# Causal attention scores as plain fp32 matmuls on quarters of the array, in tiles of 64 queries of both heads

## Chip, core and metric

The kernel runs on one core of a Trainium2 chip. The time is the device time of one execution in microseconds. The reference's tensors come in and go out in fp32, and the whole program is one launch.

Engine names are those of the profile: PE is the matmul engine (PEld its weight loads), DVE the vector engine, ACT the scalar engine, POOL GpSimd, SP the engine that issues the DMAs.

## The reference

Two attentions over 8 batches, 8 heads, 576 positions and head size 64 are added, and their sum goes into a mixture of four attention experts:

```python
def _attn_ref(q, k, v):                     # [8, 8, 576, 64]
    q_d, k_d, v_d = means of q, k, v over 4 neighbouring positions
    out_d = softmax_attention(q_d, k_d, v_d)              # 144 positions
    out_up = np.repeat(out_d, 4, axis=2)
    mask = np.abs(pos[:, None] - pos[None, :]) < 4         # a band
    out_local = softmax_attention(q, k, v, mask)
    return out_up + out_local

def _moe_ref(x, w_gate, wq, wk, wv, wo):    # x [8, 576, 512]
    logits = x @ w_gate                                    # 4 experts
    w = softmax over the two largest logits of each row
    for e in range(4):
        q, k, v = x @ wq[e], x @ wk[e], x @ wv[e]          # 64 wide
        scores = where(causal, -1e9, q @ k.T / 8)
        a = softmax(scores)
        out += (w of expert e, or 0) * (a @ v @ wo[e])
```

An expert is called a head below; the four make two pairs.

## The kernel before

Everything works on transposed data: channels on the 128 partitions, the 576 positions along the free axis.

**Stage 1** computes the first attention for a batch `b` and a chunk `c` of 128 channels (two of its eight heads). `s1_local` forms the banded scores with plain fp32 matmuls of 64 by 64 on quarters of the array (line 488), `s1_down` those of the averaged positions (546), `s1_out` transposes the softmaxes (587), multiplies with v (602, 616) and writes the sum `x` as a pair `xh`, `xl` whose sum is `x`. Both halves are in the rounded fp32 format fp32r, which the array takes in one pass.

**Stage 2** projects. `project` (645) forms q or k for one pair of heads out of three products (high by high, low by high, high by low) over four chunks, in pieces of 320 and 256 columns, into a large PSUM tile `pj`. `split` then writes q or k as two fp32r halves in SBUF: ACT casts (670), DVE subtracts (671). `s2_v` (704, 713) does v and the gate's logits, `s2_gate` the gate's weights `gw`, and `gt` for the last 64 positions, with one head on the lower and the other on the upper 64 partitions (765).

**Stage 3** is the causal attention. Queries come in tiles of 128, `i` = 0 to 3, and a tail of 64. `s2_scores` gives a tile's two heads one small PSUM tile each: three fp32r matmuls (787) of 64 by 128 for each head, on the two row halves of the array, over the `128 * (i + 1)` keys up to the diagonal block's end. `s2_scores_tail` stacks both heads' 64 queries: `s2_q_tail` (686, 688) copies them into a tile `qz` that is padded with zeros, and six matmuls on the full array (817) follow. For each head, or the tail, DVE scales, masks and takes the maximum (795, 819), ACT exponentiates and sums (793, 824), DVE adds EPS and inverts, GpSimd or DVE multiplies with the inverse and the gate's weight (802, 828). The result is in `pr0` to `pr4`, one buffer each. `s2_trans` transposes 128 by 128 blocks of it on PE (853), 25 for each batch and pair, and ACT or DVE copies them to `pta` (queries 0 to 383) and `ptb` (the others). `s2_av` (899) multiplies with v in plain fp32 on the two column halves; `s2_out` (916), and for the last batch `s2_out_cut` (940), multiply with `wo` and store.

PSUM is in two large tiles (tag `big`: projections, local scores, outputs, the tail's scores) and four small ones (tag `tr`: scores, transposes, v, products with v).

**Order.** The functions above only record operations with their costs and dependencies. `Plan.schedule` (107) simulates the engines and writes one fixed order: each engine takes the operation with the earliest due time whose inputs and buffers are there. Due times follow from the batch and stage (`CYC`, `SHIFT`) and from tables by kind (`LEAD`, `OPL`). On PE it knows four shapes of the array (`MODE`: full, `quarter`, `column`, `row`); it charges `SWC` for a change and keeps to the present shape while such an operation is due within `SWM` us of the earliest (205). Where its model expects the clock to fall, it inserts matmuls on zeros (452).

Of the kernel before, what the change touches and what calls it, by code (L numbers as in the profile page):

```python
# [319 lines left out]
def tile_attn_then_moe(ctx: ExitStack, tc: tile.TileContext, qT, kT, v, wqk, wvg, wo, out):  # L320
# [87 lines left out]
    qz = [cst.tile([128, 2, 128], F32R, name=f"qz{i}") for i in range(NQZ)]  # L408
    for t in qz:
        G.memset(t.bitcast(F32), 0.0)  # L410
    QZ = [Buf(None, None, None, None, None, None) for _ in qz]
# [255 lines left out]
    def split(kind, b, p, w0, x):  # L667
# [2 lines left out]
        op(kind + "_hi", "A", act(576), lambda: A.copy(x()[:, 0, :], ps()[:, H0:H0 + S]), r=[ps], w=[(x, 0)])  # L670
        op(kind + "_lo", "V", dve(576), lambda: V.tensor_tensor(
            x()[:, 1, :], ps()[:, H0:H0 + S], x()[:, 0, :].bitcast(F32), op=OP.subtract),
            r=[ps, (x, 0)], w=[(x, 1)])

    def s2_q(b, p):
        q = QS[b, p] = buf(wk, [128, 2, S], "q", NQ, F32R)
        split("q", b, p, 0, q)

    def s2_q_tail(b, p):

        q, z, Z = QS[b, p], qz[p % NQZ], QZ[p % NQZ]
        for e, r in enumerate(halves):
            def cp(g, e=e, r=r):
                dst, src = z[r, :, 64 * e:64 * e + 64], q()[r, :, 512:S].bitcast(F32)
                if g == "A":
                    A.copy(dst, src)
                else:
                    eng[g].tensor_copy(dst, src)
            op("q_cp", "GAV", (280, 280, 200), cp, r=[q], w=[(Z, e)])

    def s2_k(b, p):
        k = KS[b, p] = buf(wk, [128, 2, S], "k", NK, F32R)
        split("k", b, p, 256, k)
# [39 lines left out]
    def s2_gate(b):  # L733
# [23 lines left out]
        def norm():  # L757
            w, gs, cm = wt(), gst(), cmt()
            V.scalar_tensor_tensor(w, w, 1.5, cm[:, 1, :, 0, :], op0=OP.is_lt, op1=OP.mult)
            V.tensor_reduce(gs[:, 1], w, op=OP.add, axis=AX.X)  # L760
# [2 lines left out]
            V.tensor_tensor(w, w, gs[:, 2, :, None].to_broadcast([128, 5, 4]), op=OP.mult)
            for e, r in enumerate(halves):
                V.tensor_copy(gt()[r], w[hi, 4, :].rearrange("p (a e) -> p e a", e=2)[:, e])
# [2 lines left out]
        op("g_nrm", "V", 1450, norm, r=[cmt], w=[wt, gst, gt])

    PS, PT = {}, {}  # L770

    def s2_scores(b, p, i):
        m = min(128, S - 128 * i)
        n = 128 * i + m
        q, k, gw = QS[b, p], KS[b, p], GW[b]
        if i == order(b)[0]:
            s2_q_tail(b, p)
        if i == 4:
            return s2_scores_tail(b, p)
        pr, (st, ST) = buf(wk, [m, 2, n], f"pr{i}", NPR[i]), rs.next()  # L780
        pss = [small("sq") for _ in range(2)]

        def mm():
            qc = slice(128 * i, 128 * i + m)
            for x, y, one, end in ((0, 0, True, False), (1, 0, False, False), (0, 1, False, True)):
                for e, r in enumerate(halves):
                    T.matmul(pss[e]()[:m, :n], q()[r, x, qc], k()[r, y, :n], start=one, stop=end)  # L787
        op("scores", "T", dense(3, n) + 100, mm, r=[q, k], w=pss, alloc=pss + [pr])
        for e in range(2):
            ps = pss[e]  # L790

            def ex(e=e):
                A.activation(pr()[:, e, :], pr()[:, e, :], AF.Exp, bias=st[:m, e, 4:5], scale=-1.0,  # L793
                             accum_out=st[:m, e, 0:1])
            op("s_max", "V", dve(n) + 4, lambda e=e, ps=ps: V.tensor_tensor_reduce(  # L795
                pr()[:, e, :], ps()[:m, :n], causal[:, 640 - n:640], -0.125, BIG, OP.add, OP.min,
                st[:m, e, 4:5]), r=[ps], w=[(pr, e), (ST, e)])
            op("s_exp", "A", 281 + n / 1.2, ex, w=[(pr, e), (ST, e)])
        op("s_eps", "V", 70, lambda: V.tensor_reduce(st[:, :, 2], st[:, :, 0:2], op=OP.add, axis=AX.X), w=[ST])
        op("s_rec", "V", 83, lambda: V.reciprocal(st[:, :, 3], st[:, :, 2]), w=[ST])  # L800
        for e in range(2):
            op("s_nrm", "GV", (327 + n / 1.2, 189 + n / 1.92), lambda g, e=e: eng[g].tensor_scalar(  # L802
                pr()[:, e, :], pr()[:, e, :], st[:m, e, 3:4],
                gw()[:, i, 2 * p + e:2 * p + e + 1], op0=OP.mult, op1=OP.mult), r=[ST, gw], w=[(pr, e)])
        PS[b, p, i] = pr

    def s2_scores_tail(b, p):

        k, gt = KS[b, p], GT[b]
        pr, (st, ST), ps = buf(wk, [128, S], "pr4", NPR[4]), rs.next(), big("sqt")  # L810
        z = qz[p % NQZ]

        def mm():
            for n0, n1 in ((0, 320), (320, S)):
                dst = ps()[:, H0 + n0:H0 + n1]
                for x, y, one, end in ((0, 0, True, False), (1, 0, False, False), (0, 1, False, True)):
                    T.matmul(dst, z[:, x, :], k()[:, y, n0:n1], start=one, stop=end)
        op("tail", "T", dense(3, 320) + dense(3, 256) + 90, mm, r=[k, QZ[p % NQZ]], w=[ps], alloc=[ps, pr])
        op("s_max", "V", dve(S) + 4, lambda: V.tensor_tensor_reduce(
            pr(), ps()[:, H0:H0 + S], causal_t, -0.125, BIG, OP.add, OP.min, st[:, 0, 4:5]),  # L820
            r=[ps], w=[pr, ST])

        def ex():
            A.activation(pr(), pr(), AF.Exp, bias=st[:, 0, 4:5], scale=-1.0, accum_out=st[:, 0, 0:1])
        op("s_exp", "A", 281 + S / 1.2, ex, w=[pr, ST])
        op("s_eps", "V", 70, lambda: V.tensor_reduce(st[:, 0, 2:3], st[:, 0, 0:2], op=OP.add, axis=AX.X), w=[ST])
        op("s_rec", "V", 81, lambda: V.reciprocal(st[:, 0, 3:4], st[:, 0, 2:3]), w=[ST])
        op("s_nrm", "GV", (327 + S / 1.2, 189 + S / 1.92), lambda g: eng[g].tensor_scalar(
            pr(), pr(), st[:, 0, 3:4], gt()[:, p:p + 1], op0=OP.mult, op1=OP.mult), r=[ST, gt], w=[pr])
        PS[b, p, 4] = pr  # L830

    def s2_trans(b, p, i):
        pr = PS[b, p, i]
        first = []
        if i < 3 and (b, p, 0) not in PT:
            first = [buf(wk, [128, 3, 2, 384], "pta", NPA)]
            PT[b, p, 0] = first[0]
        if i >= 3 and (b, p, 1) not in PT:
            first = [buf(wk, [128, 5, 2, 192], "ptb", NPB)]
# [215 lines left out]
```

## Time and profile before

| | us |
|---|---|
| median of 3 runs | 535.25 (533.56 to 538.29) |
| the profiled execution | 535.31 |
| its span, first to last instruction | 533.4 |
| PE busy | 514.4 (96%) |
| DVE busy | 414.9 (78%) |
| ACT busy | 341.2 (64%) |
| GpSimd busy | 293.7 (55%) |
| mean granted PE clock | 0.990 |

A row of the groups names line, engine, operation, `out<-in` by tiles, shapes and count, then busy us, mean ns of one, the idle time before and who ended it. A row of the timeline or of the chain begins with its start and its length in us and ends with the number of instructions merged in it. A row of the stretches gives the busy time and the instructions of PE, PEld, DVE, ACT and POOL, then the granted PE clock, the DMA share and GB/s.

### The profile page before, as it was taken

The numbers are of one execution on the slowest core, as the hardware profiler recorded it, in microseconds if no ns is written. First come the engines' busy times: TensorE is split into PE (matmuls) and PEld (weight loads), VectorE is DVE, ScalarE is ACT, GpSimd is POOL, SyncE is SP. The second block draws the span as 40 slices with busy tenths as digits, with TensorE's granted clock in tenths as the row PEclk, the third lists the DMA queues.
The fourth block names the chain that finished last, engine by engine and source line by source line (L and its number), as shares of the span: only waits on it lengthen the run. The fifth ranks groups of instructions, "written<-read, shape, count | busy, mean of one in ns | idle before, by whom it ended". The sixth has DMA issues, their size and how long they took to land.

```text
span 533.4 us, 17338 instructions
## 1 busy us (share of the span) xinstructions
PE 514.4 (96%) x6873; PEld 451.5 (85%) x6876; DVE 414.9 (78%) x1248; ACT 341.2 (64%) x1049; POOL 293.7 (55%) x364
## 2 busy tenths in 40 slices
PE   8789989999999999999899999999999999999999
PEld 3568887888899989899798988998898887998886
DVE  6987899978886889968896966988968676537881
ACT  2886566657666656758476656776767475535773
POOL 5499966857755528765344764767474453302220
PEclk9899997999999999999999999999999999999999
DMA  8787744432343117602232323551342010200112
GB/s 208 199 228 191 174 118 116 119 94 55 111 139 93 50 26 216 183 26 68 70 118 81 113 80 106 154 141 50 98 136 70 3 36 1 77 15 12 45 47 89
DMA packets 43584, 52.77 MB, mean 99 GB/s; under 512 B 3312, under 2 KB 26352, under 8 KB 43504
## 3 DMA queue, kind: packets, MB, share of 16 engines
q1 hardware_dynamic: 43504, 51.67, 34.4%
q8 instruction: 54, 0.88, 0.7%
q14 instruction: 26, 0.21, 0.1%
HBM read 41.16 MB, written 9.44 MB: 95 GB/s over the span
## 4 chain that ended last, share of the span: by engine, by line
PE 61%; DVE 23%; POOL 5%; ACT 5%; DMA 2%; issue 2%; POOLq 0%; ACTq 0%; DVEq 0%
PE pj L645 11%; PE po L916 8%; PE o L899 7%; PE pv L704 7%; PE tq L853 6%; PE tp L587 4%; PE sq L787 4%; DVE pr L795 3%; PE o L602 3%; DMA lq<-in_qT_dram 2%; PE sc L488 2%; PE o L616 2%; DVE pr L802 2%; PE scd L546 2%; DVE lp L491 2%
## 5 line engine op out<-in xcount | busy, mean ns | idle before, releaser
L802 POOL TENSOR_SCALAR pr<-pr,pst,gw 128x384 f32<-128x384 f32 (+3 forms) x68 | 48.0, 708 | 72.8 <-DVE pst L800 51.3
L793 ACT ACTIVATE pr<-pr,pst 128x512 f32<-128x512 f32 (+3 forms) x128 | 70.8, 555 | 19.2 <-DVE pst L795 19.1
L645 PE MATMUL pj<-xh,wqk_h 128*128 128x320 f32 (+1 forms) x248 | 77.4, 312 | 0.4 <-DVE lp L491 0.3
L645 PE MATMUL pj<-xl,wqk_h 128*128 128x320 f32 (+1 forms) x248 | 73.2, 295 | 0.0
L645 PE MATMUL pj<-xh,wqk_l 128*128 128x320 f32 (+1 forms) x248 | 73.1, 295 | 0.0
L853 PE MATMUL tq<-ident,pr 128*128 128x128 f32 x400 | 58.6, 276 | 3.9 <-ACT ptb L355 1.5
L795 DVE CUSTOM_DVE_ANT_0 pr<-sq,causal 128x512 f32<-128x512 f32 (+3 forms) x128 | 57.5, 482 | 6.0 <-PE sq L787 4.5
L853 PEld LDWEIGHTS tq<-ident,pr 128*128 128x128 f32 x400 | 45.5, 141 | 8.2 <-ACT ptb L355 2.0
L509 POOL TENSOR_TENSOR lp<-lp,lst 128x640 f32<-128x640 f32 x30 | 38.4, 1283 | 20.6 <-DVE lst L508 10.7
L558 ACT ACTIVATE dp<-scd,dst 128x144 f32<-128x144 f32 x96 | 35.3, 376 | 21.1 <-DVE dst L553 16.9
L645 PEld LDWEIGHTS pj<-xh,wqk_h 128*128 128x128 f32 x248 | 46.7, 188 | 2.2 <-issue 0.6
L645 PEld LDWEIGHTS pj<-xh,wqk_l 128*128 128x128 f32 x248 | 46.8, 189 | 0.0
L645 PEld LDWEIGHTS pj<-xl,wqk_h 128*128 128x128 f32 x248 | 46.6, 188 | 0.0
L787 PE MATMUL sq<-k,q 64*128 64x128 f32 (+3 forms) x384 | 44.3, 345 | 1.2 <-DVE ol L905 0.6
L537 POOL TENSOR_TENSOR lr<-lr 72x512 f32<-72x512 f32 x31 | 40.0, 1292 | 5.0 <-DMA lr<-in_v_dram 4.9
L628 POOL TENSOR_TENSOR xl<-x,xh 128x576 fp32r<-128x576 f32 x29 | 41.4, 1426 | 0.0
L704 PE MATMUL pv<-wvg_h,xh 128*128 128x260 f32 x128 | 38.3, 299 | 1.0 <-DVE pta L357 0.4
L357 DVE COPY pt<-tp 72x384 f32<-72x384 f32 (+2 forms) x63 | 31.4, 518 | 8.6 <-PE tp L587 8.4
L602 PE MATMUL o<-pt,lv 64*64 64x58 f32 (+1 forms) x1280 | 37.0, 230 | 0.4 <-DVE x L623 0.4
L916 PE MATMUL po<-oh,wo_h 128*128 128x320 f32 (+1 forms) x112 | 36.3, 324 | 0.2 <-ACT ot L355 0.2
L704 PE MATMUL pv<-wvg_h,xl 128*128 128x260 f32 x128 | 36.2, 283 | 0.0
L704 PE MATMUL pv<-wvg_l,xh 128*128 128x260 f32 x128 | 36.1, 282 | 0.0
(160 smaller groups left out, 1506.5 us busy)
## 6 DMA issues: line engine op xcount, KB each, us to landing
lv<-in_v_dram SPq DMA_DIRECT2D x64, 160.0 KB
lq<-in_qT_dram SPq DMA_DIRECT2D x32, 292.0 KB
lk<-in_kT_dram SPq DMA_DIRECT2D x32, 292.0 KB
lr<-in_v_dram SPq DMA_DIRECT2D x32, 288.0 KB
out_dram<-ot SPq DMA_DIRECT2D x28, 288.0 KB
wst<-in_wqk_dram SPq DMA_DIRECT2D x1, 1024.0 KB
out_dram<-ot SPq DMA_DIRECT2D x4, 160.0 KB
wst<-in_wvg_dram SPq DMA_DIRECT2D x1, 520.0 KB
```

The source lines that it names most:

```text
L509: op("l_nrm", "GV", (pool_tt(n), dve(n)), lambda e: eng[e].tensor_tensor(p(), p(), st[:, :, 2:3].to_broadcast([128, NT, W]), op=OP.mult), ...
L537: G.tensor_tensor(vr()[:, :, 0:2, :], vr()[:, :, 0:2, :], vr()[:, :, 2:4, :], op=OP.add)
L602: T.matmul(o()[r, 512 * x + z:512 * x + z + n], lv()[kr, t, r], pt()[kr, t - k0, at:at + n], start=True, stop=True)
L628: op("xl", "GV", (1360, dve(576)), lambda e: eng[e].tensor_tensor(xl(), x(), xh()[:, 0:S].bitcast(F32), op=OP.subtract), r=[x, (xh, 0)], w ...
L645: T.matmul(ps()[:, H0 + n0:H0 + n1], ww[:, c, w0 + 128 * p:w0 + 128 * p + 128], xx[b, c]()[:, n0:n1], start=(i == 0), stop=(i == 3 * NP - 1))
L704: T.matmul(ps()[:, :260], xx[b, c]()[:, 128 * t:128 * t + 128], ww[:, c, :], start=(i == 0), stop=(i == 3 * NP - 1))
L787: T.matmul(pss[e]()[:m, :n], q()[r, x, qc], k()[r, y, :n], start=one, stop=end)
L793: A.activation(pr()[:, e, :], pr()[:, e, :], AF.Exp, bias=st[:m, e, 4:5], scale=-1.0, accum_out=st[:m, e, 0:1])
L795: op("s_max", "V", dve(n) + 4, lambda e=e, ps=ps: V.tensor_tensor_reduce(pr()[:, e, :], ps()[:m, :n], causal[:, 640 - n:640], -0.125, BIG, ...
L802: op("s_nrm", "GV", (327 + n / 1.2, 189 + n / 1.92), lambda g, e=e: eng[g].tensor_scalar(pr()[:, e, :], pr()[:, e, :], st[:m, e, 3:4], gw( ...
L853: T.transpose(ps()[:, 128 * x:128 * x + 128], pr()[:, c] if i == 4 else pr()[:, e, c], ident)
L916: T.matmul(ps()[:, H0 + n0:H0 + n1], ww[:, p, 128 * c:128 * c + 128], xx[b, p]()[:, n0:n1], start=(i == 0), stop=(i == 5))
```

## The change

Scores are computed for tiles of 64 queries, `t` = 0 to 8, with both heads stacked on the 128 partitions, and from q and k in plain fp32. A unit `u` = 0 to 4 holds tile 0 alone, or tiles `2u` and `2u - 1`. Each tile takes two matmuls of 64 by 64, one a head; the second tile of a unit puts its heads the other way round, so that a unit's four matmuls lie on the four quarters of the array. Tile 8 lies in a large PSUM tile, the others in small ones.

- q and k are copied from PSUM once (`q_ev`, `k_ev`, on ACT or DVE); `split`, `s2_q_tail` and `qz` go.
- `pr0` to `pr8` are constant tiles of `[128, up to 576]`. Tiles with even `t` have 64 columns more than they fill, which stay zero.
- `gt` now holds the gate's weights for all nine tiles; the normalisation always uses it.
- The transposed tiles split at 320 instead of 384; the product with v treats even and odd tiles apart, as their heads lie in opposite order.
- The output product's two column ranges, 0 to 320 and 320 to 576, wait each for its own columns.
- The planner has `scores` as `quarter`, no special tail, and other due times and parameters.

```diff
-LEAD = {..., "out": 2.1, ...}
+LEAD = {..., "out": 4.2, ...}
-OPL = {... "d_exp": -0.8, "l_rec": 1.4, "l_eps": 2.6, "vd": -4.7, "x": 7.2, "l_exp": 2.0 ...}
+OPL = {... "d_exp": -5.1, "l_rec": 4.4, "l_eps": 6.2, "vd": -2.3, "x": 10.7, "l_exp": -0.5, "k_hi": -1.3, "xt": -2.2 ...}
-WAT, NW0 = (48.0, 24.0, 63.0), 14
-LU, B0 = (1, 2, 3, 8, 10, 12, 15, 16, 24, 26, 28, 30), 2
-ORD, CUT = (2, 3, 4, 1, 0), 256
+WAT, NW0 = (53.0, 30.0, 67.0), 14
+LU, B0 = (1, 3, 8, 10, 12, 13, 16, 22, 24, 28, 29, 30), 2
+ORD, CUT = (3, 4, 2, 1, 0), 320
-LDS, LVL = 5.5, 18.5
+LDS, LVL = 5.9, 17.3
-MODE = {"local": "quarter", "down": "quarter", "o1": "quarter", "o1d": "column", "av": "column", "scores": "row"}
-SWM = {None: 16.3, "quarter": 24.5, "column": 34.1, "row": 13.2}
-SWC, SWB, MARG = 140.0, 0, 36.0
+MODE = {"local": "quarter", "down": "quarter", "o1": "quarter", "o1d": "column", "av": "column", "scores": "quarter"}
+SWM = {None: 17.4, "quarter": 24.5, "column": 34.0, "row": 17.5}
+SWC, SWB, MARG = 140.0, 0, 2.0
...
+    for t in range(NU):
+        pr.append(cst.tile([128, 128 * (t // 2 + 1) if t < NU - 1 else S], F32, name=f"pr{t}"))
...
-    def split(kind, b, p, w0, x):
-        ps = (project_by_pair if (kind, b, p) in PAIRWISE else project)(kind, b, p, w0, [x])
-        op(kind + "_hi", "A", act(576), lambda: A.copy(x()[:, 0, :], ps()[:, H0:H0 + S]), r=[ps], w=[(x, 0)])
-        op(kind + "_lo", "V", dve(576), lambda: V.tensor_tensor(
-            x()[:, 1, :], ps()[:, H0:H0 + S], x()[:, 0, :].bitcast(F32), op=OP.subtract),
...
+    def s2_q(b, p, kind="q", w0=0, to=QS, bufs=NQ):
+        x = to[b, p] = buf(wk, [128, S], kind, bufs)
         ps = (project_by_pair if (kind, b, p) in PAIRWISE else project)(kind, b, p, w0, [x])
+        op(kind + "_ev", "AV", (act(576), dve(576)), lambda e: copy(e, x(), ps()[:, H0:H0 + S]), r=[ps], w=[x])
...
-            V.tensor_tensor(w, w, gs[:, 2, :, None].to_broadcast([128, 5, 4]), op=OP.mult)
+            we = w.rearrange("p t (a e) -> p t e a", e=2)
             for e, r in enumerate(halves):
-                V.tensor_copy(gt()[r], w[hi, 4, :].rearrange("p (a e) -> p e a", e=2)[:, e])
+                for at, src, i0, i1, f in ((0, lo, 0, 4, e), (1, hi, 0, 4, 1 - e), (8, hi, 4, 5, e)):
+                    V.tensor_tensor(gt()[r, at:at + 2 * (i1 - i0) - 1:2, :], we[src, i0:i1, f, :],
+                                    gs[src, 2, i0:i1, None].to_broadcast([64, i1 - i0, 2]), op=OP.mult)
...
+    def s2_scores(b, p, u):
+        q, k, gt = QS[b, p], KS[b, p], GT[b]
+        ts, (st, ST) = unit(u), rs.next()
+        pss = [(big if t == NU - 1 else small)("sq") for t in ts]
+        def part(x, n0, n1):
+            t = ts[x]
+            at = H0 if t == NU - 1 else 0
+            for e, r in enumerate(halves):
+                T.matmul(pss[x]()[halves[e ^ x], at + n0:at + n1], q()[r, 64 * t:64 * t + 64], k()[r, n0:n1],
+                         start=True, stop=True)
+        def mm():
+            part(0, 0, min(320, 64 * ts[0] + 64))
+            if u:
+                part(1, 0, 64 * ts[1] + 64) if u == 4 else None
+                part(0, 320, 64 * ts[0] + 64) if ts[0] > 4 else None
+                part(1, 0, 64 * ts[1] + 64) if u < 4 else None
+        op("scores", "T", 107 * (ts[0] + 1) + 50, mm, r=[q, k], w=pss + [PR[t] for t in ts], alloc=pss)
+        for x, t in enumerate(ts):
...
+            op("s_nrm", "GV", (327 + n / 1.2, 189 + n / 1.92), lambda g, x=x, t=t, n=n: eng[g].tensor_scalar(
+                pr[t][:, 0:n], pr[t][:, 0:n], st[:, x, 3:4], gt()[:, t, p:p + 1], op0=OP.mult, op1=OP.mult),
+                r=[ST, gt], w=[PR[t]])
...
+    def s2_trans(b, p, u):
+        jobs = [(t, j) for t in unit(u) for j in range(t // 2 + 1)]
+        sizes = {0: (1,), 1: (3,), 2: (3, 2), 3: (4, 3), 4: (3, 2, 4)}[u]
+        part = 0 if u < 3 else 1
...
+            out = ob()[:, 0:n].rearrange("p (t q) -> p t q", q=64)
+            for par in range(2):
+                some = [t for t in tiles if t % 2 == par]
+                for j in range(some[-1] // 2 + 1):
+                    ts = [t for t in some if t // 2 >= j]
+                    for e, r in enumerate(halves):
+                        src = pt()[:, j, e ^ par, :].rearrange("p (t q) -> p t q", q=64)
+                        T.matmul(out[r, ts[0] - tiles[0]:ts[-1] - tiles[0] + 1:2, :],
+                                 vg()[:, j, 64 * (2 * p + e):64 * (2 * p + e) + 64],
+                                 src[:, ts[0] - base:ts[-1] - base + 1:2, :], start=j == 0, stop=j == some[-1] // 2)
...
+        for n0, n1 in ((0, CUT), (CUT, S)):
+            op("wo", "T", dense(6, n1 - n0), lambda n0=n0, n1=n1: mm(n0, n1),
+               r=[(x[b, p], n0) for x in (OH, OL) for p in range(2)] + needs(wo_h), w=[ps], alloc=[] if n0 else [ps, ot])
```

More of the change, by code (lines that the diff above doesn't have):

```diff
@@ L376, in tile_attn_then_moe @@
     rd = Ring(NDP, [128, 3, 5], "dst", lambda t: t[:, :, 1:2])
-    causal = cst.tile([128, 640], BF, name="causal")
-    zero = causal[:, 0:512]
+    zero = cst.tile([128, 512], BF, name="zero")
     V.memset(zero, 0.0)
@@ L407, in tile_attn_then_moe @@
     V.memset(lmask[:, NT - 1, S + PADL - SH - 4 * TQ:W], 8 * NEG)
[L408 to L411, printed above, removed]
+    pr, PR = [], []
+    for t in range(NU):
+        pr.append(cst.tile([128, 128 * (t // 2 + 1) if t < NU - 1 else S], F32, name=f"pr{t}"))
+        PR.append(Buf(None, None, None, None, None, None))
+        if t % 2 == 0 and t < NU - 1:
+            G.memset(pr[t][:, 64 * t + 64:], 0.0)
     mlt = cst.tile([128, 4, 4], F32, name="mlt")
@@ L432, in weights @@
             plan.now = at
-            tag, bufs = {id(wqk): ("pta", NPA), id(wvg): ("ptb", NPB), id(wo): ("pr3", NPR[3])}[id(src)]
+            tag, bufs = {id(wqk): ("ptb", NPB), id(wvg): ("pta", NPA), id(wo): ("wos", 1)}[id(src)]
             st = buf(wk, [128, n, m], "wst", bufs, tag=tag)
@@ L665, in project_by_pair @@
         return ps
[L667 removed]
+    def s2_q(b, p, kind="q", w0=0, to=QS, bufs=NQ):
+        x = to[b, p] = buf(wk, [128, S], kind, bufs)
         ps = (project_by_pair if (kind, b, p) in PAIRWISE else project)(kind, b, p, w0, [x])
[L670 to L689 removed]
+        op(kind + "_ev", "AV", (act(576), dve(576)), lambda e: copy(e, x(), ps()[:, H0:H0 + S]), r=[ps], w=[x])
     def s2_k(b, p):
[L692 to L693 removed]
+        s2_q(b, p, "k", 256, KS, NK)
     def s2_v(b, t):
@@ L766, in s2_gate @@
         op("g_rank", "V", 1230, rank, r=[vg], w=[wt, gst, cmt], alloc=[wt, gst, cmt, gt])
         op("g_exp", "A", 230, ex, w=[cmt])
[L768 to L781, printed above, removed]
-        def mm():
[L784 to L830, printed above, removed]
@@ L832, in s2_trans @@
-    def s2_trans(b, p, i):
-        pr = PS[b, p, i]
-        first = []
[L835 to L839, printed above, removed]
-            PT[b, p, 1] = first[0]
-        part, q0 = (0, 128 * i) if i < 3 else (1, 128 * i - 384)
-        pt = PT[b, p, part]
-        m = min(128, S - 128 * i)
-        jobs = [(j, e) for e in range(2) for j in range(i + 1)] if i < 4 else [(j, 0) for j in range(5)]
-        per = {0: 2, 1: 4, 2: 3, 3: 4, 4: 4}[i]
-        for g in range(0, len(jobs), per):
-            js = jobs[g:g + per]
+        op("g_nrm", "V", 1650, norm, r=[cmt], w=[wt, gst, gt])
@@ new lines, in s2_trans @@
+    def s2_trans(b, p, u):
+        jobs = [(t, j) for t in unit(u) for j in range(t // 2 + 1)]
+        sizes = {0: (1,), 1: (3,), 2: (3, 2), 3: (4, 3), 4: (3, 2, 4)}[u]
+        part = 0 if u < 3 else 1
+        first = []
+        if (b, p, part) not in PT:
+            first = [buf(wk, [128, 3, 2, CUT], "pta", NPA) if part == 0 else buf(wk, [128, 5, 2, S - CUT], "ptb", NPB)]
+            PT[b, p, part] = first[0]
+        pt = PT[b, p, part]
+        for size in sizes:
+            js, jobs = jobs[:size], jobs[size:]
@@ L848, in s2_trans @@
             ps = small("tq")
+            ts = sorted(set(t for t, _ in js), reverse=True)
             def tr(js=js, ps=ps):
-                for x, (j, e) in enumerate(js):
-                    c = slice(min(128 * j, S - 128), min(128 * j, S - 128) + 128)
-                    T.transpose(ps()[:, 128 * x:128 * x + 128], pr()[:, c] if i == 4 else pr()[:, e, c], ident)
-            es = sorted(set(e for _, e in js))
-            o = op("trans", "T", 109 * len(js) + 5, tr, r=[pr] if i == 4 else [(pr, e) for e in es], w=[ps],
-                   alloc=[ps] + first)
+                for x, (t, j) in enumerate(js):
+                    c = min(128 * j, pr[t].shape[1] - 128)
+                    T.transpose(ps()[:, 128 * x:128 * x + 128], pr[t][:, c:c + 128], ident)
@@ L857, in s2_trans @@
+            o = op("trans", "T", 109 * size + 5, tr, r=[PR[t] for t in ts], w=[ps], alloc=[ps] + first)
             if not first:
@@ L887, in s2_av @@
         oh, ol = OH[b, p], OL[b, p]
-        jobs, rd = [], [vg]
-        for part, (a, z) in enumerate(((0, 384), (384, S))):
-            a0, z0 = max(a, qlo), min(z, qhi)
-            if a0 < z0:
-                rd += [(PT[b, p, part], (i, g)) for i in range(5) if a0 <= 128 * i < z0 for g in range(10)]
-                js = [j for j in range(5) if 128 * j < z0]
-                jobs += [(PT[b, p, part], a, j, max(a0, 128 * j), z0, j == 0, j == js[-1]) for j in js]
-        def mm():
-            for pt, a, j, q0, q1, one, end in jobs:
-                for e in range(2):
-                    T.matmul(ob()[64 * e:64 * e + 64, q0 - qlo:q1 - qlo],
-                             vg()[:, j, 64 * (2 * p + e):64 * (2 * p + e) + 64],
-                             pt()[:, j, e, q0 - a:q1 - a], start=one, stop=end)
-        n = qhi - qlo
-        op("av", "T", cost, mm, r=rd, w=[ob], alloc=al)
+        part = int(qlo >= CUT)
+        pt, base, n = PT[b, p, part], part * CUT // 64, qhi - qlo
+        tiles = range(qlo // 64, qhi // 64)
+        cost = 30 + 110 * sum(t // 2 + 1 for t in tiles)
+        def mm():
+            out = ob()[:, 0:n].rearrange("p (t q) -> p t q", q=64)
[8 more added lines that the diff above has]
+                                 src[:, ts[0] - base:ts[-1] - base + 1:2, :], start=j == 0, stop=j == some[-1] // 2)
+        rd = [(pt, (t, j)) for t in tiles for j in range(5)]
+        op("av", "T", cost, mm, r=[vg] + rd, w=[ob], alloc=al)
         op("o_hi", "A", act(n), lambda: A.copy(oh()[:, qlo:qhi], ob()[:, :n]), r=[ob], w=[(oh, qlo)])
@@ L972, in stage3 @@
                 p, i = sched[x]
-                yield "scores", (0.35, 0.5, 0.65, 0.85, 0.8)[i], s2_scores, (b, p, i)
+                yield "scores", (0.17, 0.35, 0.55, 0.8, 1.0)[i], s2_scores, (b, p, i)
             if x > 0:
                 p, i = sched[x - 1]
-                yield "trans", (0.22, 0.44, 0.65, 0.87, 0.55)[i], s2_trans, (b, p, i)
+                yield "trans", (0.11, 0.33, 0.55, 0.76, 0.98)[i], s2_trans, (b, p, i)
                 if i in cuts:
-                    yield "av", cuts[i][2] / 1e3, s2_av, (b, p) + cuts[i]
+                    yield "av", 1.0 if cuts[i][0] == 0 else 1.8, s2_av, (b, p) + cuts[i]
         if last:
-            for n0, n1, cost in ((CUT, S, 816), (0, CUT, 653)):
+            for n0, n1, cost in ((CUT, S, 653), (0, CUT, 816)):
                 for c in range(NP):
```

71 lines of the change are left out of this document (39 added, 32 removed).

## Prediction

> **What bounds the kernel now.** I read first the engine shares and the granted clock on the page, then the busy time by stretch.
>
> ```profile
> PE 514.4 (96%) x6873; PEld 451.5 (85%) x6876; DVE 414.9 (78%) x1248; ACT 341.2 (64%) x1049; POOL 293.7 (55%) x364
> ...
> PEclk9899997999999999999999999999999999999999
> ...
> 0.00:80.00 80.00, 69.84 (x1148) 54.89 (x1151) 65.57 (x169) 51.58 (x175) 58.81 (x76) 0.97 0.75 186
> 80.00:520.00 440.00, 432.24 (x5644) 387.26 (x5644) 347.79 (x1074) 285.22 (x864) 234.41 (x287) 0.99 0.28 83
> 520.00:533.40 13.40, 12.29 (x88) 9.32 (x84) 1.59 (x5) 4.45 (x12) 0.51 (x1) 1.00 0.25 88
> ```
>
> The columns after the stretch are PE, PEld, DVE, ACT and POOL. From 80 to 520 us PE is idle for 7.76 of 440 us while DVE has 79% and ACT 65%: there the time is what PE has to do. In the first 80 us PE is idle for 10.2 us, with DVE at 82% and the DMA engines at 75%.
>
> A busy PE is not one that streams all the time, so next I read its timeline, in start times:
>
> ```profile
> 267.17 0.28 PE L916 MATMUL po<-oh,wo_l 128*128 128x256 f32 x1
> 267.28 0.28 PE L916 MATMUL po<-ol,wo_h 128*128 128x256 f32 x1
> 267.49 1.15 PE L787 MATMUL sq<-k,q 64*128 64x256 f32 x12
> 268.57 0.42 PE L645 MATMUL pj<-xh,wqk_h 128*128 128x320 f32 x1
> 268.82 0.31 PE L645 MATMUL pj<-xh,wqk_l 128*128 128x320 f32 x1
> 268.97 0.31 PE L645 MATMUL pj<-xl,wqk_h 128*128 128x320 f32 x1
> ...
> 7.26 0.34 PE L488 MATMUL sc<-lk,lq 64*64 64x64 f32 x8
> ...
> 525.92 0.39 PE L940 MATMUL po<-oh,wo_h 128*128 128x256 f32 x1
> ```
>
> L916 comes every 0.11 us, but 0.21 passes from its last to the first score matmul: 0.10 to leave a shape of the array. L645 comes every 0.15, but its second is 0.25 behind its first: 0.10 to enter one. I went through all start times and counted where the shape changes (full array, rows halved, columns halved, quarters): 232 changes, from the one at 7.26 to the one at 525.92. The runs between them are 76 full, 56 quarter, 52 column and 49 row runs. The excess over an operation's usual interval, on both sides of each change, without single excesses over 0.25 us (those are waits), sums to 37.6 us: **0.16 us a change**.
>
> **The score matmuls: 0.** From the chain of work, which shows how far each group moves PE on:
>
> ```profile
> 258.33 2.86 PE o L899 x32
> ...
> 261.70 0.59 PE sc L488 x40
> ...
> 262.51 0.50 PE scd L546 x12
> ...
> 263.71 0.48 PE sq L787 x6
> ...
> 267.56 1.08 PE sq L787 x10
> ...
> 273.12 1.17 PE sq L787 x12
> ...
> 505.58 0.80 PE sqt L817 x6
> ```
>
> Before, for a batch and pair: tile 0 is 0.48, tiles 1 and 2 are 1.08, tile 3 with another tile 0 is 1.17, the tail 0.80. Taking 0.16 for a change off the first two, the set is 0.32 + 0.92 + (1.17 - 0.48) + 0.80 = 2.73 us. After, a plain fp32 matmul has two records (L488 issues 20 matmuls and shows 40), so two passes. A unit holds two tiles on the four quarters; its time is that of the longer: 64, 192, 320, 448 and 576 columns, 1600 in all, 3200 with both passes. L488 runs four at a time: 10 rounds of 64 columns in 0.59, 0.92 ns a column. L546 has 144 columns and 4 rounds in 0.50: 0.87. L899, also plain fp32, takes 2.86 for 3200 column-passes in pieces of 64 to 384; less one change, 0.84. The new streams are of that length, so I take 0.84: 2.70 us. Over 16 sets this saves 0.5 us, which I count as 0; at L488's price it would be 2.94 and add 3.4 us in all.
>
> This rests on four matmuls side by side. L546 decides that: one matmul after another, each second pass beginning with the next one's first, would make 7 steps of 0.125, 0.87 us; the row has 0.50, four steps. [...]
>
> **Changes of shape: -5.1 us.** With quarter scores the row shape goes. Keeping the order and only renaming the 64 score operations of L787 from rows to quarters leaves 206 changes; renaming the tail too, 220 (a full-array operation among full ones becomes an island). Leaving all scores out, 168: the floor, if each found a quarter run that is there anyway. The planner holds a quarter run while its next operation is due within 24.5 us, and now has 80 more operations for such runs, so I take 200: 32 x 0.16 = 5.1 us. Ends: 220 (1.9) and 168 (10.2).
>
> **q and k not split, softmax on fewer columns: -2.0 us.** Rows of the groups:
>
> ```profile
> L671 DVE TENSOR_TENSOR q<-pj,q 128x576 fp32r<-128x576 f32 x16 | 12.0, 749 | 6.5 <-ACT q L670 6.4
> L671 DVE TENSOR_TENSOR k<-pj,k 128x576 fp32r<-128x576 f32 x16 | 12.0, 748 | 2.3 <-ACT k L670 2.2
> L670 ACT CAST q<-pj 128x576 fp32r<-128x576 f32 x16 | 10.2, 639 | 5.7 <-PE pj L645 5.6
> L355 ACT COPY ot<-po 128x576 f32<-128x576 f32 x18 | 11.5, 636 | 6.5 <-PE po L916 4.8 <-issue 1.3 <-ACT pr L793 0.2
> L795 DVE CUSTOM_DVE_ANT_0 pr<-sq,causal 128x512 f32<-128x512 f32 x32 | 21.1, 681 | 0.5 <-PE sq L787 0.3
> L795 DVE CUSTOM_DVE_ANT_0 pr<-sq,causal 128x128 f32<-128x128 f32 x32 | 8.1, 282 | 3.6 <-PE sq L787 2.2 <-POOL lp L509 1.4
> L793 ACT ACTIVATE pr<-pr,pst 128x512 f32<-128x512 f32 x32 | 22.8, 715 | 3.6 <-DVE pst L795 3.5
> L793 ACT ACTIVATE pr<-pr,pst 128x128 f32<-128x128 f32 x32 | 12.7, 397 | 6.2 <-DVE pst L795 6.2
> ```
>
> Each of 32 projections loses a cast (0.64) and a subtraction (0.75) and gains one copy (0.64): 24 us less on DVE and ACT together, and the projection's PSUM tile, one of two large ones, is free 0.75 earlier. Nine maxima, exponentials and normalisations stay for each pair, over 2880 columns instead of 3136: at (681-282)/384 = 1.04 ns that is 4.3 us of DVE, at 0.83 ns 3.4 us of ACT. All of it lies beside PE and costs or saves nothing by itself; what it can reach are PE's 7.76 us of idle time after 80 us. These rows show who ends PE's waits:
>
> ```profile
> PE tp L587 <- POOL lp L509: 3.4, 4, 1.3
> ...
> PE tq L853 <- ACT ptb L355: 1.5, 1, 1.5
> ```
>
> No single engine ends most of it, and POOL's local softmax is not touched, so I take a quarter: 2.0, between 0 and 5.
>
> **The passage at 73 to 86 us: -1.7 us.** After 21 us the clock fell once:
>
> ```profile
> 73.00:80.00 7.00, 5.50 (x97) 4.77 (x95) 6.82 (x22) 3.88 (x15) 3.87 (x5) 0.92 0.19 54
> 80.00:83.50 3.50, 3.08 (x59) 2.10 (x61) 3.37 (x11) 1.14 (x4) 1.48 (x3) 0.50 0.01 2
> 83.50:87.00 3.50, 3.50 (x58) 3.20 (x52) 2.99 (x10) 2.28 (x8) 1.37 (x2) 0.69 0.26 70
> ...
> 73.73 0.66 DVE q L671
> 74.49 0.97 DVE qz L688
> ...
> 78.03 0.74 DVE gw L759
> ```
>
> The third column from the end is the granted clock: 0.92 of 7 us, 0.50 and 0.69 of 3.5 us each, together 3.4 us of PE's time lost. Before it DVE is the chain, with q's subtraction and a copy into the padded tail tile: 1.63 us that go. Whether PE's load then stays high enough to hold the clock the trace can't say: half of 3.4. Ends: all of it, or a second such fall, +3.4.
>
> **The rest on PE: +0.5 us.** Transposes stay 25 a pair. The product with v has 28 matmuls instead of 16, the same 1600 columns; 24 more passes at a few ns (0.92 against 0.84 ns on 64 columns is 5 ns a pass) are 0.1 us a pair, partly hidden: 0.5 to 2. The copies of transposed tiles go from 8 to 10 a pair on ACT or DVE, hidden by their slack; uncovered, 32 x 0.3. Memsets, constants and the new due times cost nothing: they lie in the first 60 us, behind the loads. The output product now waits for its own columns of both pairs alone, which can only start it earlier.
>
> **Gates: 0, but see the rivals.** The normalisation of the gates loses a product and two copies and gains six products on 64 partitions:
>
> ```profile
> L763 DVE TENSOR_TENSOR gw<-gw,gs 128x20 f32<-128x20 f32 x8 | 2.3, 293 | 0.3
> L765 DVE COPY gt<-gw 64x2 f32<-64x2 f32 x16 | 3.8, 240 | 0.4
> ```
>
> Six at 0.24 to 0.29 less 0.77 make 0.7 to 1.0 us a batch on DVE.
>
> **Sum.** The profiled execution took 535.31 us (span 533.4), the median is 535.25: the same. 535.3 - 5.1 - 2.0 - 1.7 + 0.5 = **527.0 us**, 1.5% less.
>
> **Rivals.**
> - *Reshaping doesn't fall.* Score units are released by the four small PSUM tiles, not by what the array is doing; 49 row runs for 64 operations speak for that. Then 220 changes remain, the idle time moves elsewhere, and with the copies uncovered nothing is left: 531 to 537.
> - *All of it comes.* 168 to 180 changes, the clock holds, 4 us of idle time close: 535.3 - 9.5 - 4 - 3.4 = 518.
> - *The gates take over, slower.* Until now only the tail needed the rearranged gates; now all nine tiles do, so the first normalisation comes 6 x 0.27 - 0.29 = 1.3 us later wherever it waits for the gates. DVE works through the products in order, with the maxima queued behind them; ACT, the transposes and PE wait in turn. The chain at 73 to 79 us runs through the gates already. If all eight batches wait: +10.6, less 1.9 for the least reshaping: 544. It decides as soon as a unit's sums are ready before the last gate product; against it speaks that PE's waits name the gates only once, for 0.6 us:
>
> ```profile
> PE sq L787 <- DVE gs L760: 0.6, 1, 0.6
> ```
>
> [...]
>
> **Numbers.** Less than 1%, 5.4 us, is about what a measurement tells from no change here. Forecast, 523 to 529.9: 0.38. All of it, below 523: 0.20. No fall, 530 to 540.6: 0.23. Gates: 0.16. Order: 0.03. So faster 0.58, same 0.23, slower 0.19. The range goes from 516, the gain with the floor of 168 changes and the idle time nearly closed, to 544, the gates' price.
>
> **What would show it.** Right: no 64-row by 128-column matmul is left; about 200 changes of shape; a pair's score units move PE by about 2.7 us beside the changes; the clock stays at 1.0 from 20 us on; DVE and ACT are together 20 to 30 us less busy. Wrong: score rows that take over 3.2 us a pair; PE idle over 8 us between 80 and 520; waits of transposes on the gates or on the normalisation; a second dip of the clock.

## Result and the profile after

The changed kernel takes 521.1 us (median), against 534.7 for the kernel before in four runs: 0.9725 of the time before by the means (95% interval 0.9663 to 0.9787). One of its own four runs took 795.9 us; that slow run is left out of the ratio. Forecast were 527.0 us and a range of 516 to 544. The profiled execution has a span of 519.5 us, 13.9 less than before.

The engine shares and the granted clock on its page:

```profile
PE 503.0 (97%) x7468; PEld 447.8 (86%) x7468; DVE 392.0 (75%) x1256; ACT 331.2 (64%) x1049; POOL 276.4 (53%) x346
...
PEclk9899998999999999999999999999999999999999
```

The busy time by stretch (PE, PEld, DVE, ACT, POOL, then clock, DMA share, GB/s):

```profile
0.00:80.00 80.00, 72.44 (x1273) 57.11 (x1273) 67.03 (x183) 49.62 (x167) 63.10 (x84) 0.98 0.78 194
80.00:508.00 428.00, 420.01 (x6120) 382.78 (x6121) 324.49 (x1073) 277.99 (x873) 213.33 (x263) 1.00 0.29 84
508.00:519.50 11.50, 10.58 (x78) 7.93 (x76) 0.49 (x1) 3.62 (x9) 0.00 (x0) 1.00 0.30 104
```

PE is busy 11.4 us less, DVE 22.9, ACT 10.0 and POOL 17.3 less. PE's idle time in the middle stretch has not fallen: 8.0 of 428 us, against 7.8 of 440.

Counted from PE's start times as in the prediction, the changes of shape fell from 232 to 176 (66 full, 63 quarter and 48 column runs), their excess from 37.9 to 27.7 us; excesses over 0.25 us, the waits, from 22.7 to 19.5. (The first figure was 37.6 in the prediction, without three single operations between two changes.) The numbers of changes are firm; the sizes depend on what is taken as an operation's usual interval. With the median of each group's intervals the excess falls by 7 us instead of 10. From one start to the next, all score matmuls move PE by 50.1 us in all, before by 42.0 for the tiles and 14.2 for the tails.

The second fall of the clock is still there, half as long:

```profile
78.00:82.00 4.00, 2.50 (x53) 1.79 (x49) 3.91 (x18) 3.07 (x13) 3.34 (x4) 0.93 0.76 218
82.00:86.00 4.00, 3.91 (x77) 2.33 (x73) 3.17 (x11) 2.69 (x8) 3.37 (x6) 0.65 0.69 168
```

7% and 35% of 4 us are 1.7 us lost, against 3.4 before.

This accounting puts half to three quarters of the gain (7 to 10 of 13.6 us) on the changes of shape. But the chain of work says something else beside it. Its shares by engine, first of the kernel before, then of the changed one:

```profile
PE 61%; DVE 23%; POOL 5%; ACT 5%; DMA 2%; issue 2%; POOLq 0%; ACTq 0%; DVEq 0%
```

```profile
PE 74%; DVE 20%; ACT 3%; issue 2%; POOL 1%; ACTq 0%; DVEq 0%; POOLq 0%
```

DVE has a fifth to a quarter of the chain, though PE is 96% busy. So there are three candidates for the cause that the experiments can separate: fewer changes of shape, less work on DVE, and the new tables of the planner.

### The profile page after: what moved, and what is told of

It is laid out like the page before. It is cut to its first block, busy times and chain, and to the rows that moved or that the text cites. A ratio compares the mean times of both kernels' runs of the same rounds, so it can differ in the third digit from the quotient of the medians.

```text
span 519.5 us, 18547 instructions
## 1 busy us (share of the span) xinstructions
PE 503.0 (97%) x7468; PEld 447.8 (86%) x7468; DVE 392.0 (75%) x1256; ACT 331.2 (64%) x1049; POOL 276.4 (53%) x346
## 4 chain that ended last, share of the span: by engine, by line
PE 74%; DVE 20%; ACT 3%; issue 2%; POOL 1%; ACTq 0%; DVEq 0%; POOLq 0%
PE pj L647 15%; PE pv L687 8%; PE o L854 8%; PE tq L815 8%; PE po L871 7%; PE sq L770 6%; PE tp L589 5%; PE o L604 3%; DVE pr L783 3%; PE o L618 2%; PE sc L490 2%; PE scd L548 2%; DVE lp L493 2%; DVE pr L794 2%; PE pv L696 2%
## 5 line engine op out<-in xcount | busy, mean ns | idle before, releaser
L794 POOL TENSOR_SCALAR pr<-pr,pst,gt 128x64 f32<-128x64 f32 (+8 forms) x86 | 59.6, 699 | 105.2 <-DVE pst L791 40.5
L786 ACT ACTIVATE pr<-pr,pst 128x384 f32<-128x384 f32 (+7 forms) x144 | 80.0, 556 | 33.0 <-DVE pst L783 32.4
L647 PE MATMUL pj<-xh,wqk_h 128*128 128x320 f32 (+1 forms) x248 | 76.6, 309 | 1.4 <-DVE lp L493 0.6
L783 DVE CUSTOM_DVE_ANT_0 pr<-sq,causal_t 128x384 f32<-128x384 f32 (+7 forms) x144 | 66.3, 481 | 12.4 <-PE sq L770 12.0
L647 PE MATMUL pj<-xl,wqk_h 128*128 128x320 f32 (+1 forms) x248 | 73.2, 295 | 0.0
L647 PE MATMUL pj<-xh,wqk_l 128*128 128x320 f32 (+1 forms) x248 | 73.1, 295 | 0.0
L770 PE MATMUL sq<-k,q 64*64 64x320 f32 (+5 forms) x704 | 56.7, 397 | 0.1
L647 PEld LDWEIGHTS pj<-xh,wqk_h 128*128 128x128 f32 x248 | 46.6, 188 | 4.3 <-DVE x L625 1.3
L647 PEld LDWEIGHTS pj<-xh,wqk_l 128*128 128x128 f32 x248 | 46.7, 188 | 0.0
L647 PEld LDWEIGHTS pj<-xl,wqk_h 128*128 128x128 f32 x248 | 46.6, 188 | 0.0
L511 POOL TENSOR_TENSOR lp<-lp,lst 128x640 f32<-128x640 f32 x29 | 37.0, 1278 | 16.5 <-DVE lst L510 14.0
L860 DVE TENSOR_TENSOR ol<-o,oh 128x320 fp32r<-128x320 f32 (+1 forms) x32 | 14.6, 456 | 34.7 <-ACT oh L859 34.4
L770 PEld LDWEIGHTS sq<-k,q 64*64 64x64 f32 x704 | 29.0, 134 | 11.2 <-DVE pst L783 1.0
L604 PEld LDWEIGHTS o<-pt,lv 64*64 64x64 f32 x1280 | 30.9, 135 | 7.1 <-issue 3.1
L630 POOL TENSOR_TENSOR xl<-x,xh 128x576 fp32r<-128x576 f32 x26 | 36.9, 1421 | 0.0
L359 DVE COPY pt<-tp 72x384 f32<-72x384 f32 (+2 forms) x57 | 28.5, 515 | 11.2 <-PE tp L589 11.0
```

The lines of the kernel that those rows point to most:

```text
L511: op("l_nrm", "GV", (pool_tt(n), dve(n)), lambda e: eng[e].tensor_tensor(p(), p(), st[:, :, 2:3].to_broadcast([128, NT, W]), op=OP.mult), ...
L604: T.matmul(o()[r, 512 * x + z:512 * x + z + n], lv()[kr, t, r], pt()[kr, t - k0, at:at + n], start=True, stop=True)
L630: op("xl", "GV", (1360, dve(576)), lambda e: eng[e].tensor_tensor(xl(), x(), xh()[:, 0:S].bitcast(F32), op=OP.subtract), r=[x, (xh, 0)], w ...
L647: T.matmul(ps()[:, H0 + n0:H0 + n1], ww[:, c, w0 + 128 * p:w0 + 128 * p + 128], xx[b, c]()[:, n0:n1], start=(i == 0), stop=(i == 3 * NP - 1))
L770: T.matmul(pss[x]()[halves[e ^ x], at + n0:at + n1], q()[r, 64 * t:64 * t + 64], k()[r, n0:n1], start=True, stop=True)
L783: op("s_max", "V", dve(n) + 4, lambda x=x, t=t, n=n, src=src: V.tensor_tensor_reduce(pr[t][:, 0:n], src(), causal_t[:, S - n:S], -0.125, B ...
```

## Experiments

Times are medians of several runs; a ratio is to the kernel before, on the same chip. Each chip's kernel before had a median of 533.0 to 534.7 us. Changes, excess and waits (both in us) are from start times, as above, in the one profiled execution of each kernel.

| kernel | us | ratio (95%) | changes | excess | waits |
|---|---|---|---|---|---|
| before | 534.7 | 1 | 232 | 37.9 | 22.7 |
| changed | 521.1 | 0.973 (0.966-0.979) | 176 | 27.7 | 19.5 |
| e1 quarter | 526.3 | 0.983 (0.977-0.990) | 176 | 27.3 | 25.0 |
| e2 full | 532.6 | 0.997 (0.995-0.999) | 306 | 49.7 | 13.8 |
| e3 second copies | 527.8 | 0.987 (0.983-0.991) | 176 | 27.0 | 25.9 |
| e4 old tables | 533.1 | 0.998 (0.996-1.000) | 194 | 29.2 | 28.8 |
| e5 before, new tables | 540.9 | 1.012 (1.007-1.017) | 246 | 39.6 | 26.3 |
| e6 before, moved | 543.6 | 1.017 (1.011-1.024) | 243 | 39.6 | 28.8 |
| e7 changed, moved | 539.7 | 1.010 (1.007-1.013) | 192 | 29.0 | 33.5 |
| e8 gates | 527.9 | 0.987 (0.982-0.992) | 176 | 27.9 | 24.4 |
| e9 before, moved again | 545.4 | 1.022 (1.017-1.027) | 242 | 38.2 | 29.6 |
| e10 changed, moved again | 528.2 | 0.990 (0.985-0.995) | 182 | 28.6 | 28.0 |
| e11 light | 514.7 | 0.966 (0.961-0.971) | 176 | 27.2 | 17.8 |
| e12 refit | 520.5 | 0.976 (0.971-0.981) | 176 | 27.4 | 20.2 |

### What a change of shape costs: e1 and e2

e1, ahead of a score unit's matmuls:

```diff
+            T.matmul(pss[0]()[lo, H0:H0 + 64] if ts[0] == NU - 1 else pss[0]()[lo, 0:64], zero[lo, 0:64], zero[lo, 0:64], start=True, stop=True)
             part(0, 0, min(320, 64 * ts[0] + 64))
```

> The changed kernel with one bf16 matmul of zeros on one quarter (64 by 64, 64 columns) ahead of each of the 80 score units; it writes columns that the unit then overwrites, and the order is the same. Control for the next run. All theories: 80 x 0.03 to 0.06 us, so 521 to 526.

e2, the same on the full array:

```diff
+            T.matmul(pss[0]()[:, H0:H0 + 64] if ts[0] == NU - 1 else pss[0]()[:, 0:64], zero[:, 0:128], zero[:, 0:64], start=True, stop=True)
             part(0, 0, min(320, 64 * ts[0] + 64))
```

> The same with the matmul of zeros on the full array, so that a quarter run is broken ahead of the unit: in the written order 61 units follow a quarter operation (two changes of shape more), 8 a column operation (one more), 11 a full one (none): 130 more. Theory 'changes of shape are the gain', 0.16 us each: 21 us above the control, 543 to 547. Rival 'the gain is relief of DVE and ACT, PE would only have waited': less than 8 us above the control.

The control lost 5 us, but in the profiled execution not by its matmuls: the first projection of batch 0 (L662) began 4 us later, long before the first matmul of zeros at 66.7 us. Its rows in the view of that line, of the changed kernel, e1 and e2; the second time is the first start:

```profile
L662 PE MATMUL pj<-xh,wqk_h x8: 279/294/413, 40.6 to 46.0; 128*128 128x320 f32 x4, 128*128 128x256 f32 x4
```

```profile
L662 PE MATMUL pj<-xh,wqk_h x8: 279/292/416, 44.6 to 49.9; 128*128 128x320 f32 x4, 128*128 128x256 f32 x4
```

```profile
L662 PE MATMUL pj<-xh,wqk_h x8: 279/292/421, 41.0 to 46.5; 128*128 128x320 f32 x4, 128*128 128x256 f32 x4
```

From there to the end of the span it is 478.9 us in the changed kernel, 524.0 - 44.6 = 479.4 in e1 and 530.7 - 41.0 = 489.7 in e2. So the matmuls themselves cost 0.5 us, 0.006 each against the 0.03 to 0.06 of the expectation, which was an estimate, and 130 changes cost **10.3 us, 0.08 each**, in which lies also what a full matmul takes more than a quarter one. This rests on one execution each; the fastest runs of e1 and e2, 520.6 and 531.3, are 10.7 apart. By the medians, the measure set beforehand, the difference is 6.3, with late starts of the control in it: that is under the rival's 8. By either measure the theory's 21 us are out, by half or more.

The excess did rise, by 22 us in the table's count and by 19 with the groups' medians: 0.15 to 0.17 a change. The rest was made up elsewhere. The table's count finds it in waits, which fell by 11; with the medians it lies in intervals too short to count as waits. That PE came later to work that then was ready fits both, but is not shown by itself.

```profile
PE 83%; DVE 13%; ACT 2%; issue 1%; POOL 0%; DVEq 0%; ACTq 0%; POOLq 0%
```

In e2's chain DVE's share is down to 13%, from 20% in the changed kernel: where PE is slower, DVE gives less of the length.

### What DVE's work costs: e3 and e11

e3 gives DVE a second copy behind each copy of q or k:

```diff
+        def ev(e):
+            copy(e, x(), ps()[:, H0:H0 + S])
+            V.tensor_copy(x(), ps()[:, H0:H0 + S])
-        op(kind + "_ev", "AV", (act(576), dve(576)), lambda e: copy(e, x(), ps()[:, H0:H0 + S]), r=[ps], w=[x])
+        op(kind + "_ev", "AV", (act(576), dve(576)), ev, r=[ps], w=[x])
```

> The changed kernel with a second copy of q and k on DVE behind the first, for each of 32 projections: 24 us of DVE and 0.8 us more from a projection to its scores, as the split had; order and changes of shape as in the changed kernel. Theory 'changes of shape': 521 to 526, DVE work lies beside PE. Rival 'relief of DVE and ACT': most of the gain goes, 529 to 535.

527.8, 6.6 above the changed kernel, between the two. The rows of the second copies:

```profile
L675 DVE COPY k<-pj 128x576 f32<-128x576 f32 x16 | 12.1, 756 | 8.4 <-ACT k L357 8.1
L675 DVE COPY q<-pj 128x576 f32<-128x576 f32 x16 | 12.1, 755 | 12.2 <-ACT q L357 11.8
```

As the copies came late in a fixed order, this alone could be the order's disturbance. e11 goes the other way, with the order as it is; it leaves out half of each sum and maximum, so it does not compute the result:

```diff
-... V.tensor_reduce(st[:, :, 0], p(), op=OP.add, axis=AX.X)
+... V.tensor_reduce(st[:, :, 0], p()[:, :, 0:W:2], op=OP.add, axis=AX.X)
-... scs[x]()[:, 0:n * SD].rearrange("p (t w) -> p t w", w=SD),
+... scs[x]()[:, 0:n * SD].rearrange("p (t w) -> p t w", w=SD)[:, :, 0:SD:2],
```

> The changed kernel with less work on DVE and the order as it is: the sum of the banded softmax and the maximum of the averaged one are taken over every second column only (the other half is left out), 64 and 32 instructions of half the length: about 20 us less of DVE, as q and k not being split took off. Theory 'relief of DVE is worth little, its work lies beside PE; the second copies cost because they came late in a fixed order': 518 to 521. Rival 'DVE's work sets the time': 513 to 516.

514.7: 6.4 less, the rival's number. The groups and the chain of e11, with the two groups of the changed kernel first:

```profile
L508 DVE TENSOR_REDUCE lst<-lp 128x10 f32<-128x640 f32 x32 | 25.8, 808 | 2.9 <-ACT lp L507 2.4 <-ACT lp L501 0.5
...
L552 DVE TENSOR_REDUCE scd<-scd 128x2 f32<-128x288 f32 x64 | 24.1, 381 | 3.4 <-PE scd L548 3.1
```

```profile
L552 DVE TENSOR_REDUCE scd<-scd 128x2 f32<-128x144 f32 x64 | 17.1, 269 | 4.7 <-PE scd L548 4.1
L508 DVE TENSOR_REDUCE lst<-lp 128x10 f32<-128x320 f32 x32 | 15.2, 475 | 3.2 <-ACT lp L507 2.7 <-ACT lp L501 0.4
```

```profile
PE 76%; DVE 15%; ACT 4%; issue 2%; DMA 1%; POOL 1%; SPq 0%; ACTq 0%; DVEq 0%; POOLq 0%
```

17.6 us less on these two groups gave 6.4 us; 24 us more (32 x 0.75) cost 6.6: **about 0.3 us for 1 us of DVE, in both directions**, at the same 176 changes. The price is rough. e11 ran where the kernel before took 533.0 instead of 534.7 us; set against the kernel before on the same chip, e11 gains 4.7 and e3 loses 7.1 us, 0.27 and 0.30 for 1 us. And DVE's busy time as a whole moved less than the groups, by 14.6 and 19.0 us; by it the prices are 0.32 to 0.44. The intervals of e11 and the changed kernel touch. But both signs hold, and my theory falls here: DVE's work doesn't lie beside PE. The chain had said as much. 20% of 519.5 us are 104 of DVE's 392 busy us, 0.27 of each.

### The planner's tables: e4, e5, e6, e7, e9, e10

e4 is the changed kernel with `LEAD`, `OPL`, `WAT`, `LU`, `SHIFT`, `LDS`, `LVL`, `SWM` and `MARG` of before; e5 is the kernel before with the new ones.

> The changed kernel with the due times and planner constants of before (all tables but the order of the last batch and its cut). The written order has 193 changes of shape instead of 175. Theory 'changes of shape': 18 x 0.17 = 3 us more, 523 to 526. Rival 'the new tables are the gain, not the quarters': 531 to 536.

> The kernel before with the due times and planner constants of the changed one (all tables but the order of the last batch and its cut); 245 changes of shape in the written order instead of 231. Theory 'tables fit one code only; the quarters give what is left at equal fit': worse than before, 537 to 545. Rival 'the new tables are better for any code and are the gain': 520 to 528.

e4 lost 12 of the 13.6 us; the rival's number. Yet e5 is 1.2% slower than before, so the new tables aren't better in themselves. e6 and e9 (before) and e7 and e10 (changed) move each entry of `OPL` by a random amount of at most 0.3 us, which is enough for another order; in e7:

```diff
-OPL = {"s_nrm": 3.2, "l_nrm": 4.2, "t_ev": 1.0, "tp_ev": 6.1, ...}
+OPL = {"s_nrm": 3.042, "l_nrm": 3.962, "t_ev": 0.938, "tp_ev": 5.893, ...}
```

> The kernel before with each entry of OPL moved by a random amount of at most 0.3 us: the fit of its tables is spoiled, nothing else (242 changes of shape instead of 231). Theory 'tables fit one code only': 538 to 545, and about 10 above the changed kernel with spoiled or old tables (533). Rival 'the tables of before are no special fit': 533 to 537, and the changed kernel with old tables at 533 says that the quarters give nothing.

> The changed kernel with each entry of OPL moved by a random amount of at most 0.3 us (191 changes of shape instead of 175). Theory 'tables fit one code only': 527 to 534, like the run with the old tables. Rival 'the new tables are good in a wide surrounding': 520 to 524.

> The kernel before with another random movement of OPL by at most 0.3 us (241 changes of shape). So far spoiled tables gave 540.9 and 543.6 for the kernel before, 533.1 and 539.7 for the changed one: 5.9 apart in the means, 13 with fitted tables. Theory 'at equal fit the quarters give about 8, the rest of the 13 is the fit': 539 to 545. Rival 'the fit is all': the same as the next run within 2 us.

> The changed kernel with another random movement of OPL by at most 0.3 us (181 changes of shape). Theory 'at equal fit the quarters give about 8': 530 to 537, with the excess at changes of shape near 28 us and the rest of the loss in PE's waits. Rival 'the fit is all': the same as the run before within 2 us.

e7 was slower than expected, e10 faster, e9 just above its bound. With tables not made for the code the kernel before takes 540.9, 543.6 and 545.4, the changed one 533.1, 539.7 and 528.2: means of 543.3 and 533.7, **9.6 apart** (standard error 3.6 from three and three). With their own tables they are 13.6 apart. All three of the changed kernel lie below all three of the kernel before. So the change probably holds without the fit; from three and three, a 95% interval would still reach 0. The fit is worth about as much as the change: 9 us on the kernel before, 13 on the changed one. It can be seen where: among the kernels before the excess at changes is 38 to 40 us, among the changed ones 27 to 29, fitted or not; what the fit takes away are waits, 23 and 19 us instead of 26 to 34.

### Gates: e8

```diff
-            for e, r in enumerate(halves):
+            for e, r in [x for x in enumerate(halves) for _ in range(2)]:
```

> The changed kernel with the six gate products done twice on DVE, so that every normalisation of a batch may start 1.4 us later; same order. Rival of the prediction 'the gates' chain sets the time': 8 x 1.4 = 11 us more, 530 to 533. Theory 'it lies beside PE': 521 to 524.

527.9, 6.8 more, for 6.4 us of DVE:

```profile
L749 DVE TENSOR_TENSOR gt<-gw,gs 64x8 f32<-64x8 f32 (+1 forms) x96 | 12.8, 160 | 1.7
```

One product takes 0.16 us, so the delay was 1.0 a batch, not 1.4. The loss is as long as the work, but in the profiled execution it came almost whole through the clock, which fell twice more, each time to 0.66 over 5 us, 1.7 us lost, and longer after 82 us:

```profile
82.00:90.00 8.00, 7.06 (x106) 4.92 (x107) 7.18 (x28) 5.52 (x16) 6.70 (x10) 0.57 0.53 139
143.00:148.00 5.00, 4.43 (x22) 4.01 (x23) 4.23 (x12) 3.41 (x14) 4.19 (x6) 0.66 0.46 138
198.00:203.00 5.00, 5.00 (x114) 4.37 (x114) 3.76 (x10) 2.68 (x13) 2.66 (x3) 0.66 0.60 172
```

43% of 8 us are 3.4 us lost in the first of these rows, against 1.7 in the changed kernel: together 5.1 us more. From the first projection, at 42.0 us, to the end e8 takes 484.4 us, 5.5 more than the changed kernel. That leaves 0.4 us beside the clock. The mean granted clock is 0.984 to 0.990 in all four runs of e8 and 0.993 to 0.997 in three of the changed kernel, so the falls belong to e8 and not to one execution. The gates hold up POOL's normalisation in four places in both kernels (9.6 us in all, 13.3 in e8), not in every batch, and no wait of PE is put down to them.

### Another fit: e12

e12 has other values in `OPL`, `LEAD`, `SHIFT`, `SWM` and `LU`.

> The changed kernel with other due times, planner constants and choice of local softmaxes, found by a random search for the earliest end in the planner's own model (2.2 us earlier than for the changed kernel; 175 changes of shape). Theory 'the fit to the planner's model is worth what it says': 518 to 521. Rival 'a gain of 2 us in the model is drowned by what it leaves out': 521 to 530.

520.5, within the first theory's bounds; its interval of 0.971 to 0.981 can't be told from that of the changed kernel. No version here that computes the whole result is clearly faster.

## Why the prediction was right, and where it was off

**Direction and range** held: faster, 521.1 within 516 to 544, by 2.5% (medians) to 2.75% (means) instead of 1.5%. But 521.1 lies below the band of 523 to 529.9 that had the greatest chance; the rival "All of it comes", with a chance of 0.20, had the nearest number, 518. Of its conditions the 176 changes came, while the clock fell again and PE's idle time didn't close. The sum fell 5.3 us short of the gain, nearly all of it in the term for DVE.

**Score matmuls, 0.** Right as far as it can be told: 50.1 us instead of 56.2, both with the changes among them; no run has the streams alone. The quarters work side by side, and more freely than assumed. Two cuts of the changed kernel's PE groups by shape, at the start of a unit that is issued as 320, 128, then 384 columns:

```profile
L770 PE MATMUL sq<-k,q 64*64 64x384 f32 x2 | 0.5, 533 | 0.0
L770 PE MATMUL sq<-k,q 64*64 64x320 f32 x2 | 0.5, 480 | 0.0
```

```profile
L770 PE MATMUL sq<-k,q 64*64 64x384 f32 x4 | 0.9, 508 | 0.0
L770 PE MATMUL sq<-k,q 64*64 64x320 f32 x2 | 0.4, 429 | 0.0
L770 PE MATMUL sq<-k,q 64*64 64x128 f32 x4 | 0.4, 269 | 0.0
```

In the first, 135.80 to 135.85 us, the 384 columns of the second tile run beside the first 320; the 128, which stand ahead of them in the program, come only in the second cut, 136.30 to 136.55. So matmuls on different quarters started out of program order here. "Order", to which 0.03 went, stands for quarters that wait for each other; it is out.

**Changes of shape, -5.1.** The sum's term had two errors that cancel, by luck. 56 changes went instead of 32, because the planner found a quarter run for most score units: of the 63 quarter runs only 10 hold scores alone (the floor was 168). And a change is worth 0.08 us to the end, not the 0.16 that I read off PE: 56 x 0.08 = 4.5. The 0.16 is about right as an interval (0.15 to 0.17 in e2), but half of it doesn't reach the end.

**q and k not split, fewer columns, -2.0 (0 to 5).** This term was too small: 22.9 us less on DVE at 0.3 are 6.9. (At 0.32 to 0.44, the prices by DVE's whole busy time, they are 7 to 10.) Not all of the 22.9 is the split: 24.0 us of subtractions went, but 17 of the 32 copies came to DVE and took 12.7, and some other work moved to other engines in the new order. The step that failed is "what it can reach are PE's 7.76 us of idle time". In e11 PE's idle time fell by 1.5 us, from 16.5 to 15.0 over the span, and PE's busy time by 5.3, with the same matmuls:

```profile
PE 497.7 (97%) x7465; PEld 446.2 (87%) x7468; DVE 377.4 (74%) x1256; ACT 331.4 (65%) x1049; POOL 276.8 (54%) x346
```

1.7 us of the 5.3 are a fall of the clock that e11 doesn't have: its mean granted clock is 0.997, that of the changed kernel 0.993. So busy time holds lost clock; the other 3.6 us I take for waits between instructions that are too short for the idle column, which no row shows singly. The share of DVE in the chain would have given the price: 23% of 533.4 are 123 of 414.9 us, 0.30 of each, 6.8 us for 22.9.

**Clock, -1.7.** 1.7 us lost instead of 3.4. The guess of half was met by luck, for the sign of being right, a clock at 1.0 from 20 us on, was not, and the falls vary from version to version at one written order: in e3 there is only one, before 80 us (mean clock 0.997), in e8 two more than in the changed kernel. That PE's load holds the clock was an estimate that no run shows: in e8 the clock was 0.66 from 198 to 203 us, with PE busy for all of the 5 us.

**Rest of PE, +0.5.** The product with v moves PE by 47.1 us before and after: 0.

**Due times, 0.** The sentence that they "cost nothing" is furthest from what the runs showed: with the old ones the kernel takes 12 us more. I priced where the loads lie, not that an order is written once for given durations. As the kernel before had tables of its own too, how much of the 13.6 us is a better fit stays open: at spoiled tables 9.6 remain, give or take several us.

**Gates, 0.** In the changed kernel their cost is inside the net result. The rival's price of 1.3 us a batch was too high: six products are 1.0. Its mechanism, a chain in which all eight batches wait, is not what e8 shows: there the loss came through the clock.

By these prices the gain is 4.5 + 6.9 + 1.7 = 13.1 of 13.6 us, but prices from single disturbances of one order don't have to add up, and the cost of the gate products in the changed kernel and the gains of ACT and POOL are in no experiment alone; POOL's share of the chain fell from 5% to 1%. What the split of q and k gives by itself, apart from the eight per cent fewer columns, stays open.

## What to carry to other kernels

An engine that is 96% busy need not be the only one that sets the time. A first price for work off that engine is its engine's time in the chain of work divided by its busy time (0.27 to 0.30 here, 0.27 to 0.44 measured); check it by a run with less of that work and one with more, and look at the clock in both. A cost read off the busiest engine's intervals can be too high: here half of it reached the end. Where the order is written by a planner with tuned tables, compare two versions at spoiled tables too, several each: one fitted pair says as much of the fit as of the change, and three spoiled ones each were hardly enough.
